# One list for the order of the first phase's products, and new durations for its small steps, in a fused attention and two-layer network kernel

## The chip, the core and the metric

The kernel runs on one core of one Trainium2 chip. A core has five engines with an instruction queue each: PE (TensorE, matrix products), DVE (VectorE), ACT (ScalarE), POOL (GpSimd) and SP (SyncE, which here only issues DMA transfers). Results of PE land in PSUM; the other engines take them from there into SBUF. The metric is the device time of one execution in microseconds (us); lower is better.

## What is computed

Eight batches of eight heads with 576 positions of 64 numbers; 32 packing rows per head. All data are 32-bit floats. Weights come as 64-bit numbers and are decoded on the chip.

```python
def sm_attn(qq, kk, vv):
    s = scale * np.matmul(qq, kk.transpose(0, 1, 3, 2))
    s = s - np.max(s, axis=-1, keepdims=True)
    a = np.exp(s)
    a = a / (np.sum(a, axis=-1, keepdims=True) + 1e-09)
    return np.matmul(a, vv)
p_packed = sm_attn(p, k, v)
out = sm_attn(q, p_packed, p_packed)          # then x: 4608 tokens x 512
...
h = np.maximum(np.maximum(x @ w1, x @ w2), x @ w3)     # 512 x 768 weights
x = h @ w_out                                          # 768 x 512
...
h = x @ w_in                                           # 512 x 2048
P = a[0] + a[1] * h + a[2] * h2 + a[3] * h3            # h2 = h*h, h3 = h2*h
Q = 1.0 + np.abs(b[0]) * np.abs(h) + np.abs(b[1]) * h2
out = (P / (Q + 1e-06)) @ w_out                        # 2048 x 512
```

## The kernel before

There are two phases. The second phase (lines 826 to 908) is the last layer, `psh` and `po` in the profile; the change does not touch it. The first phase does attention and the layer before it, and all its steps go through a planner.

**Steps of the first phase.** A unit `u` is one half batch of four heads; there are 16, four to a block `bp`. Each letter below is one small program step of `do()`:

- `S u` (`s_stage`, matrix products at line 469): scores of packing rows against k; then maximum, exponential and sums on DVE, ACT and POOL.
- `T u` (`a_stage`, line 513): four transposes of those weights. `V u` (`v_stage`, lines 532, 535 and, one transpose, 545): their product with v, which gives `ppk`, the packed rows.
- `s u` (`s2_stage`, line 560): scores of q against `ppk`, and their softmax on DVE, POOL and ACT, which ends in `a2h` and `a2l`, a high and a low part.
- `m` (`m_stage`, line 607): the packed rows times a 128-column piece of w1, w2 or w3, for two units; ACT and DVE split it in `mh` and `ml`. 48 of them. It needs the weight tile `wt`: in block 0 decoded from `w_raw` by DVE, ACT and POOL (lines 342 to 370), in later blocks loaded back from `w_scr`.
- `y` (`y_piece`, lines 59 to 61): twelve products of 288 columns, `a2` with `m`. 144 of them; three make one step of the maximum over w1, w2 and w3 (`hm`, lines 630 and 632), which `y_end` splits in `hh` and `hl`.
- `x` (`x2_stage`, lines 59 to 61 on `wo_h`): 36 products with w_out; 32 of them, the last eight outside the planner.
- `o`, `w`: decoding of a piece of w_out and of the second phase's weights.

**Two shapes on PE.** `y`, `x`, the transposes and the fillers use the whole 128x128 array. `S`, `s` and `m` use it as 64x32 tiles, the products with v as 128x32 tiles. Below, `S`, `s` and `m` are called tiled products; a run of tiled products with no whole-array product between them is called a visit to the tiled shape, and a tiled product that follows another one directly is called joined to it.

**What sets the order.** The steps are recorded in the order of a text of such letters, made by `text(bp)` from a table of places and by `m_next()`, which puts `m` a fixed number of steps ahead. `Plan.rate` gives every operation a due time from this order (for PE the sum of the durations before it). `Plan.run` then places operations on five modelled engines by readiness and due time; a PE operation may go ahead of the order by at most `AHEAD` = 12 us of due time. Durations (`us`) and a charge for a change of shape are numbers in the source. Where the modelled PE would wait over 0.3 us in the first 140 us, `keep_warm` puts transposes of an identity there, the fillers (line 285). PSUM holds two tiles `psy` (for `y`, `x` and fillers) and two tiles `pst` (for all small steps); `mh` and `ml` have four buffers each. What comes out is a fixed order for each engine.

Of the kernel before, what the change touches and what calls it, by code (L numbers as in the profile page):

```python
# [31 lines left out]
def attn_moe_moe2_kernel(  # L32
# [113 lines left out]
    class Plan:  # L146
# [51 lines left out]
        def run(self):  # L198
# [19 lines left out]
            for _ in range(len(self.ops)):  # L218
# [27 lines left out]
                op.eng, op.us = e, us  # L246
                if e == "PE":
                    if m != mode:
                        t, mode = t + 0.09, m
                    end = t + us + 0.18  # L250
                    free[e] = t + us
                elif e == "SP":
                    dma = max(dma, t + 2.7) + op.kb / 406.0
                    end, free[e] = dma, t + 0.45
                else:
                    if m == "two":
                        held[e] = t + us
                    end = t + us
                    free[e] = end - 0.08
# [33 lines left out]
    add = plan.add  # L293
# [6 lines left out]
    def flat(wt):  # L300
        return wt().rearrange("p a b -> p (a b)")[:, :768]

    def load_raw(src, up=0.0):

        n = src.shape[1]
        b = Buf(wp, [128, 768, 2] if wide else [128, 768], I32 if wide else F32, "w_raw", NRAW)

        def go():
            raw = b()[:, :n]
            nc.sync.dma_start(raw.rearrange("p n w -> p (n w)") if wide else raw, src.bitcast(I32) if wide else src)  # L310

        add("SP", 0, go, w=[b], kb=n, up=up)
        return b, n

    def decode(loaded, single, tiles, key):
# [72 lines left out]
    def w_decode(f, g, loaded):  # L388

        b = wt_buf()  # L390
        decode(loaded, True, lambda: (None, flat(b)), b)
        add("SP", 0, lambda: nc.sync.dma_start(w_scr[f, g], flat(b)), r=[b], w=[("w_scr", f, g)], kb=384)
        return b

    def w_load(f, g):

        b = wt_buf()
        add("SP", 0, lambda: nc.sync.dma_start(flat(b), w_scr[f, g]), r=[("w_scr", f, g)], w=[b], kb=384)
        return b
# [58 lines left out]
    def s_stage(u, kt):  # L458
# [33 lines left out]
                pool.tensor_tensor(out=s[a : a + 64, 3:4], in0=s[a : a + 64, i : i + 1], in1=s[a : a + 64, 2:3],  # L492
                                   op=ALU.add)

        add("PE", 0.58, mm, r=[kt, "pt"], w=[ps, e], mode="t")
        add("DVE", 0.75, lambda: dve.tensor_reduce(out=mx()[:, 0:2], in_=ps()[:, :, :288], axis=AX.X, op=ALU.max),
            r=[ps], w=[mx], up=OUT)
        add("DVE", 0.4, lambda: swap(dve), r=[mx], w=[mx], up=OUT, other={"POOL": (0.4, lambda: swap(pool), "two")})
# [6 lines left out]
    def a_stage(e):  # L505

        ps, at, ax = ps_buf("pst"), Buf(kp, [128, 4, 128], F32, "at", 2, False), Buf(kp, [128, 2, 32], F32, "ax", 3, False)

        def mm():
            for i in range(2):  # L510
                for c in range(2):
                    o = 320 * i + 128 * c
                    pe.transpose(ps()[:, 0, 256 * i + 128 * c : 256 * i + 128 * c + 128], e()[:, o : o + 128], ident)

        add("PE", 0.5, mm, r=[e], w=[ps, at])
        add("ACT", 0.6, lambda: act.copy(at().rearrange("p a b -> p (a b)"), ps()[:, 0]), r=[ps], w=[at], up=OUT)
        add("DVE", 0.2, lambda: dve.transpose(ax().rearrange("p a b -> p (a b)"), e()[:, 256:320]), r=[e], w=[ax])
        return at, ax

    def v_stage(u, at, vt, sm):  # L520
# [13 lines left out]
            for h in range(4):  # L534
                pe.matmul(pv[32 * h : 32 * h + 32, :64], lhsT=ax()[:, h // 2], rhs=vt()[:, 16 + h], start=False, stop=True)

        add("PE", 0.57, mm, r=[at, ax, vt], w=[ps], mode="v")

        def two():
            return ps()[:, 0, :64].unsqueeze(1).to_broadcast([128, 2, D])  # L540
# [9 lines left out]
    def s2_stage(u, qt, a2):  # L550
# [24 lines left out]
        def wide_of(t):  # L575
            return t().unsqueeze(2).to_broadcast([128, 18, 32])

        add("PE", 0.58, mm, r=[qt, ("ppk", u // 4 % 2, u % 4)], w=[ps, tb], mode="t")
        add("DVE", 0.9, turn, r=[ps], w=[tb], up=OUT)
        add("DVE", 0.75, lambda: dve.tensor_reduce(out=mx(), in_=t0(), axis=AX.X, op=ALU.max), r=[tb], w=[mx])  # L580
        add("POOL", 1.35, lambda: pool.tensor_tensor(out=t0(), in0=t0(), in1=wide_of(mx), op=ALU.subtract),
# [13 lines left out]
    def m_stage(bp, b2, wts):  # L595

        ps = ps_buf("pst")
        hi, lo = (Buf(mp, [128, 2, 384], F32R, f"m{x}", 4) for x in "hl")  # L600

        def mm():
            for g in range(2):
                for h in range(4):
                    i, j = divmod(h, 2)
                    l, c = slice(64 * j, 64 * j + 64), 32 * (h ^ g)
                    pe.matmul(ps()[c : c + 32, g, :384], lhsT=ppk[l, bp % 2, 2 * b2 + g, 32 * h : 32 * h + 32],  # L607
                              rhs=flat(wts[g])[l, 384 * i : 384 * i + 384], start=True, stop=True)

        add("PE", 0.74, mm, r=[*wts, ("ppk", bp % 2, 2 * b2), ("ppk", bp % 2, 2 * b2 + 1)], w=[ps, hi, lo], mode="t")  # L610
        add("ACT", 0.8, lambda: act.copy(hi(), ps()[:, :, :384]), r=[ps], w=[hi], up=OUT)
        add("DVE", 0.95, lambda: dve.tensor_tensor(out=lo(), in0=ps()[:, :, :384], in1=hi().bitcast(F32), op=ALU.subtract),
            r=[ps, hi], w=[lo], up=OUT)
        return hi, lo
# [60 lines left out]
    def a2_of(bp):  # L675
        return a2s.setdefault(bp, [[None, None], [None, None]])

    def m_next(n=1):
        for bp, f, b2 in m_seq[len(made) : len(made) + n]:
            if any(4 * bp + 2 * b2 + g not in vs for g in range(2)):  # L680
                break
            if (bp, f) not in wts:
                wts[bp, f] = [w_load(f, g) if bp else w_decode(f, g, load_raw(w123[2 * f + g], RUP.get(2 * f + g, 0.0))) for g in range(2)]
            ms[bp, f, b2] = m_stage(bp, b2, wts[bp, f])
            made.append((bp, f, b2))

    def y_steps():
        for bp in range(NBP):
            for k, (f, b2) in enumerate(YS[bp]):
                hm, h = hm_buf(), [Buf(hp_pool, [128, S], F32R, f"h{x}{b2}{f}") for x in "hl"]  # L690
                hs[bp][b2][f] = h
                for w in range(3):
                    if w == 1:
                        m_next(max(0, 12 * bp + min(k + MA, 12) - len(made)))
                    y_piece(w, ms[bp, f, b2], a2_of(bp)[b2], hm, h)
                    if w == 2:
                        y_end(hm, h)
                    yield
# [33 lines left out]
            if i is not None:  # L732
                w2_decode(i, load_raw(w_2[i]))

    def text(bp):
        at_ = {}

        def put(k, what):
            at_.setdefault(k, []).append(what)

        if bp + 1 < NBP:
            for u in range(4):
                for k, d in (("S", 0), ("T", 2), ("V", 3)):
                    put(PK[bp][u] + d, f"{k}{4 * bp + 4 + u}")
                put(S2AT[bp][u], f"s{4 * bp + 4 + u}")
            for k in MX[bp]:
                put(k, "m")
        for k in OAT if bp == 0 else WAT[bp]:
            put(k, "w" if bp else "o")
        out = START.split() if bp == 0 else []  # L750
        n = 36 - out.count("y")
        for k in range(36 - n, 44 if bp + 1 < NBP else 36):
            out += ["y" if k < 36 else "x"]
            out += at_.get(k, [])
        return out

    MA = 3
    RUP = {}
    START = "S0 S1 T0 T1 V0 V1 s0 s1 m S2 S3 T2 T3 V2 V3 s2 s3 m m"
    PK = [(16, 23, 30, 36), (2, 9, 16, 23), (2, 9, 16, 23)]  # L760
    S2AT = [(36, 37, 40, 41), (36, 37, 39, 40), (36, 37, 39, 40)]
    MX = [(38, 39)] * 3
    OAT = (28, 34, 37, 39)
    WAT = [(), (1, 5, 9, 13, 17, 21, 25, 29, 33, 36, 39, 41), (1, 5, 9, 13, 17, 21, 25, 29, 33, 36, 39, 41), (1, 5, 9, 13, 17, 21, 25, 29)]
    for bp in range(NBP):
        for what in text(bp):
            do(what)
    bp, hs = NBP - 1, hs[NBP - 1]

# [190 lines left out]
```

## Time and profile before

| | |
|---|---|
| median of 3 runs | 1319.13 us (1319.11 to 1319.16) |
| the profiled execution's own time | 1319.51 us |
| its span, first to last instruction | 1317.7 us |
| PE busy in the span | 1301.6 us, 99% |
| first `y` product starts | 41.18 us |
| first product of the second phase starts | 519.21 us |

The profile is of one execution. Spans, durations and waits are those of the hardware profiler; L469 is line 469 of the kernel. "Idle before" is the time that an engine stood still ahead of an instruction, and the arrow names what ended it. Ends of PE's products are modelled, since products are pipelined: one of 288 columns is shown as 0.29 us long while the next starts after 0.13 us.

### The profile page before, as it was taken

How to read it: one execution, taken by the hardware profiler on the slowest of the kernel's cores; microseconds unless marked ns; L12 is line 12 of the kernel's file. 1: busy time of each engine (PE TensorE's matmuls, PEld its weight loads, DVE VectorE, ACT ScalarE, POOL GpSimd, SP SyncE). 2: the span in 40 equal slices, each digit the busy share in tenths (PEclk: the TensorE clock that was granted, in tenths of full speed). 3: DMA queues.
4: the chain of work that ended last, by engine and by line, in shares of the span. 5: the costliest groups of instructions: out<-in, count | busy, mean ns of one | idle time of the engine just before them, and what ended most of it. 6: DMA issues, size and time to landing. Idle time of an engine off the chain costs nothing.

```text
span 1317.7 us, 21701 instructions
## 1 busy us (share of the span) xinstructions
PE 1301.6 (99%) x8582; PEld 1095.1 (83%) x8582; DVE 1059.4 (80%) x1652; ACT 798.5 (61%) x1346; POOL 218.0 (17%) x215
## 2 busy tenths in 40 slices
PE   9999999999999999999999999999999999999998
PEld 7878888998889899788888888888888888888886
DVE  6899878867886741999788888888897888888877
ACT  4465545435534422777668677686686776866765
POOL 4744523333233200001001010010010100100000
PEclk9999999999999999999999999999999999999999
DMA  9657656666646448501002001020020010100000
GB/s 377 255 192 250 211 193 233 227 216 217 228 134 231 139 165 312 218 6 43 17 0 64 1 17 49 0 64 1 0 65 0 17 41 0 56 1 0 33 1 33
DMA packets 52006, 141.92 MB, mean 108 GB/s; under 512 B 5568, under 2 KB 5568, under 8 KB 51136
## 3 DMA queue, kind: packets, MB, share of 16 engines
q1 hardware_dynamic: 51616, 140.01, 30.6%
q8 instruction: 67, 1.10, 0.3%
q10 hardware_dynamic: 288, 0.52, 0.1%
q14 instruction: 35, 0.29, 0.1%
HBM read 100.14 MB, written 40.37 MB: 107 GB/s over the span
## 4 chain that ended last, share of the span: by engine, by line
PE 75%; ACT 1%; DMA 1%; DVE 0%; issue 0%; POOL 0%; ACTq 0%
PE po L59 10%; PE po L60 10%; PE po L61 10%; PE psh L59 10%; PE psh L60 10%; PE psh L61 10%; PE psy L59 5%; PE psy L60 5%; PE psy L61 5%; PE pst L607 1%; DMA wt<-w_scr 0%; DMA w_scr<-wt 0%; PE pst L560 0%; PE pst L532 0%; DMA out_dram<-ob 0%
## 5 line engine op out<-in xcount | busy, mean ns | idle before, releaser
L59 PE MATMUL psh<-xh,wi_b 128*128 128x512 f32 x576 | 224.3, 390 | 1.0 <-issue 1.0
L60 PE MATMUL psh<-xl,wi_b 128*128 128x512 f32 x576 | 224.8, 391 | 0.0
L61 PE MATMUL psh<-xh,wi_b 128*128 128x512 f32 x576 | 224.4, 390 | 0.0
L59 PE MATMUL po<-wq_b,gh 128*128 128x512 f32 x540 | 212.2, 393 | 0.8 <-ACT gh L52 0.8
L60 PE MATMUL po<-wq_b,gh 128*128 128x512 f32 x540 | 211.2, 391 | 0.0
L850 ACT ACTIVATE hb<-psh,babs 128x512 f32<-128x512 f32 (+1 forms) x145 | 100.1, 690 | 177.7 <-PE psh L61 177.7
L853 DVE SCALAR_TENSOR_TENSOR hb<-h,babs,hb 128x512 f32<-128x512 f32 (+1 forms) x145 | 108.2, 746 | 97.3 <-ACT h L851 97.0
L61 PE MATMUL po<-wq_b,gl 128*128 128x512 f32 x540 | 182.2, 391 | 0.0
L59 PE MATMUL psy<-a2h,mh 128*128 128x288 f32 x576 | 177.4, 308 | 4.7 <-ACT hh L642 1.8
L60 PE MATMUL psy<-a2l,mh 128*128 128x288 f32 x576 | 169.8, 295 | 0.0
L61 PE MATMUL psy<-a2h,ml 128*128 128x288 f32 x576 | 169.7, 295 | 0.0
L56 POOL TENSOR_TENSOR xl<-xr,xh 128x512 fp32r<-128x512 f32 x28 | 37.0, 1320 | 641.8 <-ACT xh L52 641.8
L59 PEld LDWEIGHTS psy<-a2h,mh 128*128 128x128 f32 x576 | 108.2, 188 | 32.8 <-issue 10.9
L59 PEld LDWEIGHTS psh<-xh,wi_b 128*128 128x128 f32 x576 | 108.1, 188 | 24.6 <-issue 1.2
L61 PEld LDWEIGHTS psh<-xh,wi_b 128*128 128x128 f32 x576 | 108.1, 188 | 23.0
L60 PEld LDWEIGHTS psh<-xl,wi_b 128*128 128x128 f32 x576 | 108.2, 188 | 23.0
L61 PEld LDWEIGHTS po<-wq_b,gl 128*128 128x128 f32 x540 | 101.3, 188 | 23.8
L59 PEld LDWEIGHTS po<-wq_b,gh 128*128 128x128 f32 x540 | 101.4, 188 | 22.9 <-ACT gh L52 1.2
L60 PEld LDWEIGHTS po<-wq_b,gh 128*128 128x128 f32 x540 | 101.4, 188 | 22.4
L52 ACT CAST gh<-u 128x512 fp32r<-128x512 f32 (+1 forms) x145 | 90.7, 626 | 41.7 <-DVE u L860 40.4
L59 PE MATMUL psy<-hh,wo_h 128*128 128x288 f32 x384 | 115.4, 300 | 0.0
L858 DVE SCALAR_TENSOR_TENSOR u<-u,av,h 128x512 f32<-128x512 f32 (+1 forms) x145 | 108.7, 750 | 7.7 <-ACT h L855 7.6
(105 smaller groups left out, 2726.6 us busy)
## 6 DMA issues: line engine op xcount, KB each, us to landing
w_raw<-in_w_dram SPq DMA_DIRECT2D x32, 512.0 KB, 4.7
w_scr<-wt SPq DMA_DIRECT2D x32, 512.0 KB, 3.9
wt<-w_scr SPq DMA_DIRECT2D x36, 384.0 KB, 4.1
vraw<-in_v_dram SPq DMA_DIRECT2D x16, 640.0 KB, 5.3
kt<-in_k_dram SPq DMA_DIRECT2D x16, 576.0 KB, 6.1
w_raw<-in_w_dram SPq DMA_DIRECT2D x12, 768.0 KB, 8.5
kt<-in_q_dram SPq DMA_DIRECT2D x16, 576.0 KB, 6.0
x_scr<-hm SPq DMA_DIRECT2D x32, 288.0 KB, 3.3
```

What stands on the lines that cost most here:

```text
L52: act.copy(hi, src)
L56: e.tensor_tensor(out=lo, in0=src, in1=hi.bitcast(F32), op=ALU.subtract)
L59: pe.matmul(out_ap, lhsT=lh, rhs=rh, start=first, stop=False)
L60: pe.matmul(out_ap, lhsT=lh, rhs=rl, start=False, stop=False)
L61: pe.matmul(out_ap, lhsT=ll, rhs=rh, start=False, stop=last)
L607: pe.matmul(ps()[c : c + 32, g, :384], lhsT=ppk[l, bp % 2, 2 * b2 + g, 32 * h : 32 * h + 32], rhs=flat(wts[g])[l, 384 * i : 384 * i + 384] ...
L850: act.activation(hb, h, AF.Abs, scale=babs[:, 0:1])
L853: dve.scalar_tensor_tensor(out=hb, in0=h2, scalar=babs[:, 1:2], in1=hb, op0=ALU.mult, op1=ALU.add)
L858: dve.scalar_tensor_tensor(out=u, in0=u, scalar=av[:, 0:1], in1=h2, op0=ALU.add, op1=ALU.mult)
```

## The change

The places, the table and `text(bp)` go; in their stead stands one list of letters for the whole phase, `TEXT`, which a search program found by moving small steps about in the planner's model. `y_steps` no longer puts `m` in by itself, since the list holds all of them. The durations of seven kinds of PE steps in the model are set anew, and leaving the tiled shape has a charge of its own. Arithmetic, tiles, buffers and the second phase stay as they were.

```diff
                 if e == "PE":
                     if m != mode:
-                        t, mode = t + 0.09, m
+                        t += (0.13 if mode == "t" else 0.0) + (0.09 if m else 0.11)
+                        mode = m
...
-        add("PE", 0.58, mm, r=[kt, "pt"], w=[ps, e], mode="t")
+        add("PE", 0.51, mm, r=[kt, "pt"], w=[ps, e], mode="t")
...
-        add("PE", 0.5, mm, r=[e], w=[ps, at])
+        add("PE", 0.55, mm, r=[e], w=[ps, at])
...
-        add("PE", 0.57, mm, r=[at, ax, vt], w=[ps], mode="v")
+        add("PE", 0.6, mm, r=[at, ax, vt], w=[ps], mode="v")
...
-        add("PE", 0.58, mm, r=[qt, ("ppk", u // 4 % 2, u % 4)], w=[ps, tb], mode="t")
+        add("PE", 0.51, mm, r=[qt, ("ppk", u // 4 % 2, u % 4)], w=[ps, tb], mode="t")
...
-        add("PE", 0.74, mm, r=[*wts, ("ppk", bp % 2, 2 * b2), ("ppk", bp % 2, 2 * b2 + 1)], w=[ps, hi, lo], mode="t")
+        add("PE", 0.67, mm, r=[*wts, ("ppk", bp % 2, 2 * b2), ("ppk", bp % 2, 2 * b2 + 1)], w=[ps, hi, lo], mode="t")
...
-    def m_next(n=1):
-        for bp, f, b2 in m_seq[len(made) : len(made) + n]:
...
+    def m_next():
+        bp, f, b2 = m_seq[len(made)]
...
-            for k, (f, b2) in enumerate(YS[bp]):
+            for f, b2 in YS[bp]:
+                while (bp, f, b2) not in ms:
+                    m_next()
...
-                    if w == 1:
-                        m_next(max(0, 12 * bp + min(k + MA, 12) - len(made)))
...
-    START = "S0 S1 T0 T1 V0 V1 s0 s1 m S2 S3 T2 T3 V2 V3 s2 s3 m m"
-    PK = [(16, 23, 30, 36), (2, 9, 16, 23), (2, 9, 16, 23)]
...
+    TEXT = (
+        "S0 S1 T0 T1 V0 V1 m s0 S2 s1 S3 T3 T2 V3 V2 m s2 s3 m y m y y y m y m y y y y y S4 S6 m y y y y m y y y y y y",
...
+    for line_ in TEXT:
+        for what in line_.split():
             do(what)
```

Three places show what this moves. Lines of the changed file are one higher than before in this part (608 is 607 of before).

The first place is PE from just ahead of the first `y` to the wait in front of the thirteenth `y` before, and to the like wait after. L560 (561) is `s`, L607 (608) is `m`, L285 (286) a filler, L59 to L61 are `y`. Before:

```order
L560 MATMUL pst<-kt,ppk 32x288 x8
L545 MATMUL pst<-ident,zt 128x128
L285 MATMUL psy<-ident 128x128 x5
L560 MATMUL pst<-kt,ppk 32x288 x8
L285 MATMUL psy<-ident 128x128 x42
L59 MATMUL psy<-a2h_618,mh 128x288
...
L607 MATMUL pst<-wt,ppk 32x384 x16
L285 MATMUL psy<-ident 128x128 x42
```

After:

```order
L561 MATMUL pst<-kt,ppk 32x288 x16
L286 MATMUL psy<-ident 128x128 x12
L608 MATMUL pst<-wt,ppk 32x384 x16
L286 MATMUL psy<-ident 128x128 x13
L608 MATMUL pst<-wt,ppk 32x384 x8
L286 MATMUL psy<-ident 128x128 x9
L59 MATMUL psy<-a2h_647,mh 128x288
...
L286 MATMUL psy<-ident 128x128 x7
L608 MATMUL pst<-wt,ppk 32x384 x8
```

Ahead of the first `y` stand four `m` (32 instructions at L608 in all, one of the four further up) where one stood, and 209 fillers where 204 stood. After the first `y` stand 7 fillers, now after the sixth `y`, where 42 stood after the twelfth.

The second place is PE in the course of block 0, where S of the next block's units stands among `y` (L469, now L470). Before:

```order
L61 MATMUL psy<-a2h_906,ml 128x288
L469 MATMUL pst<-kt,pt 32x288 x8
L59 MATMUL psy<-a2h_618,mh 128x288
...
L61 MATMUL psy<-a2h_684,ml 128x288
L469 MATMUL pst<-kt,pt 32x288 x8
L59 MATMUL psy<-a2h_618,mh 128x288
```

After:

```order
L61 MATMUL psy<-a2h_751,ml 128x288
L470 MATMUL pst<-kt,pt 32x288 x8
L608 MATMUL pst<-wt,ppk 32x384 x8
L59 MATMUL psy<-a2h_647,mh 128x288
...
L61 MATMUL psy<-a2h_935,ml 128x288
L608 MATMUL pst<-wt,ppk 32x384 x16
L59 MATMUL psy<-a2h_955,mh 128x288
```

An `S` and an `m`, or two `m`, now go in one visit to the tiled shape. From the first `y` on there were 4 tiled products joined to another tiled one, and there are 26.

The third place is DVE around the first `y`. `dec_r`, `dec_t` and `wt` are the decoding of w1 to w3, `a2l` is what the first `y` waits for, `ml` belongs to an `m`, `hm` to a `y`. Before:

```order
L354 SCALAR_TENSOR_TENSOR wt<-w_raw,dec_r 128x768
L636 TENSOR_TENSOR a2l_685<-hm,a2h_684 128x576
L580 TENSOR_REDUCE mx_704<-e 128x18
L345 TENSOR_SCALAR dec_r<-w_raw 128x768
L632 TENSOR_TENSOR hm<-psy,hm 128x576
```

After:

```order
L613 TENSOR_TENSOR ml<-pst,mh 128x768 x2
L637 TENSOR_TENSOR a2l_752<-hm,a2h_751 128x576
L346 TENSOR_SCALAR dec_r<-w_raw 128x768
L343 TENSOR_SCALAR dec_t<-w_raw 128x768 x2
L355 SCALAR_TENSOR_TENSOR wt<-w_raw,dec_r 128x768
L346 TENSOR_SCALAR dec_r<-w_raw 128x768
L363 SCALAR_TENSOR_TENSOR dec_t<-w_raw,dec_t 128x768 x2
L633 TENSOR_TENSOR hm<-psy,hm 128x576
```

Nearly all of the fifth and sixth weight tiles' decoding on DVE now stands ahead of the first `hm` of a `y`; before, it began there and went on past the sixth `hm`.

## Rows read from the trace of the kernel before

**Rows 1.** Busy time of each engine by stretch of the span (us, instructions), granted PE clock.

```profile
0.00:41.20 41.20, 38.38 (x529) 30.45 (x529) 29.62 (x64) 18.20 (x39) 20.99 (x36) 1.00 0.97 385
41.20:126.00 84.80, 80.22 (x836) 68.67 (x834) 76.32 (x106) 48.94 (x81) 47.09 (x40) 1.00 0.62 218
126.00:250.00 124.00, 123.56 (x1294) 107.25 (x1293) 98.87 (x169) 61.04 (x110) 42.04 (x47) 1.00 0.63 211
519.20:1317.70 798.50, 791.68 (x3456) 648.54 (x3456) 673.27 (x1021) 561.88 (x935) 36.96 (x28) 1.00 0.10 33
```

**Rows 2.** Timeline of PE (start, length): one `m` alone, two `m` joined.

```profile
78.42 0.29 PE L60 MATMUL psy<-a2l,mh 128*128 128x288 f32 x1
78.55 0.29 PE L61 MATMUL psy<-a2h,ml 128*128 128x288 f32 x1
78.77 0.88 PE L607 MATMUL pst<-wt,ppk 64*32 64x384 f32 x16
79.57 0.40 PE L59 MATMUL psy<-a2h,mh 128*128 128x288 f32 x1
79.81 0.29 PE L60 MATMUL psy<-a2l,mh 128*128 128x288 f32 x1
...
44.32 0.29 PE L61 MATMUL psy<-a2h,ml 128*128 128x288 f32 x1
44.54 1.52 PE L607 MATMUL pst<-wt,ppk 64*32 64x384 f32 x32
45.99 0.40 PE L59 MATMUL psy<-a2h,mh 128*128 128x288 f32 x1
46.23 0.30 PE L60 MATMUL psy<-a2l,mh 128*128 128x288 f32 x1
```

**Rows 3.** Timeline of PE: the two long stretches of fillers.

```profile
36.62 4.80 PE L285 MATMUL psy<-ident 128*128 128x128 f32 x42
41.18 0.38 PE L59 MATMUL psy<-a2h,mh 128*128 128x288 f32 x1
...
66.59 4.80 PE L285 MATMUL psy<-ident 128*128 128x128 f32 x42
71.15 0.38 PE L59 MATMUL psy<-a2h,mh 128*128 128x288 f32 x1
```

**Rows 4.** All waits of PE, 41 to 519 us: total, times, longest.

```profile
PE psy L59 <- ACT hh L642: 1.8, 1, 1.8
PE psy L59 <- ACT hm L630: 1.6, 5, 0.7
PE psy L59 <- DVE hm L632: 1.2, 2, 0.8
PE pst L513 <- ACT e L483: 0.5, 1, 0.5
PE pst L532 <- ACT at L516: 0.3, 1, 0.3
```

**Rows 5.** Timeline of PE in the first 20 us, idle time in brackets.

```profile
1.42 4.32 PE L285 MATMUL psy<-ident 128*128 128x128 f32 x19 [1.42 <-POOL ident masks.py:199]
...
8.16 0.72 PE L469 MATMUL pst<-kt,pt 64*32 64x288 f32 x16 [0.73 <-DMA kt<-in_k_dram]
...
19.74 0.71 PE L560 MATMUL pst<-kt,ppk 64*32 64x288 f32 x13 [0.46 <-issue]
```

**Rows 6.** Timeline of DVE: one decoding step, twice.

```profile
61.14 0.95 DVE L354 SCALAR_TENSOR_TENSOR wt<-w_raw,dec_r 128x768 f32<-128x768 uint32 x1
...
64.40 2.19 DVE L354 SCALAR_TENSOR_TENSOR wt<-w_raw,dec_r 128x768 f32<-128x768 uint32 x1
```

**Rows 7.** Timeline of POOL at the same time.

```profile
64.35 1.42 POOL L636 TENSOR_TENSOR hl<-hm,hh 128x576 fp32r<-128x576 f32 x1
```

**Rows 8.** Groups of instructions: busy us, mean ns, idle before. What empties an `m`.

```profile
L612 DVE TENSOR_TENSOR ml<-pst,mh 128x768 fp32r<-128x768 f32 x48 | 45.5, 950 | 19.9 <-ACT mh L611 19.8
L611 ACT CAST mh<-pst 128x768 fp32r<-128x768 f32 x48 | 38.3, 800 | 25.1 <-PE pst L607 24.8
```

More of the change, by code (lines that the diff above doesn't have):

```diff
@@ L301, in flat, with load_raw @@
         return wt().rearrange("p a b -> p (a b)")[:, :768]
-    def load_raw(src, up=0.0):
+    def load_raw(src):
         n = src.shape[1]
@@ L310, in go @@
             nc.sync.dma_start(raw.rearrange("p n w -> p (n w)") if wide else raw, src.bitcast(I32) if wide else src)
-        add("SP", 0, go, w=[b], kb=n, up=up)
+        add("SP", 0, go, w=[b], kb=n)
         return b, n
@@ L676, in a2_of @@
         return a2s.setdefault(bp, [[None, None], [None, None]])
-    def m_next(n=1):
-        for bp, f, b2 in m_seq[len(made) : len(made) + n]:
[L680 to L685, printed above, removed]
+    def m_next():
+        bp, f, b2 = m_seq[len(made)]
+        assert all(4 * bp + 2 * b2 + g in vs for g in range(2))
+        if (bp, f) not in wts:
+            wts[bp, f] = [w_load(f, g) if bp else w_decode(f, g, load_raw(w123[2 * f + g])) for g in range(2)]
+        ms[bp, f, b2] = m_stage(bp, b2, wts[bp, f])
+        made.append((bp, f, b2))
     def y_steps():
         for bp in range(NBP):
-            for k, (f, b2) in enumerate(YS[bp]):
+            for f, b2 in YS[bp]:
+                while (bp, f, b2) not in ms:
+                    m_next()
                 hm, h = hm_buf(), [Buf(hp_pool, [128, S], F32R, f"h{x}{b2}{f}") for x in "hl"]
@@ L733, in do @@
                 w2_decode(i, load_raw(w_2[i]))
[L735 to L758, printed above, removed]
-    START = "S0 S1 T0 T1 V0 V1 s0 s1 m S2 S3 T2 T3 V2 V3 s2 s3 m m"
-    PK = [(16, 23, 30, 36), (2, 9, 16, 23), (2, 9, 16, 23)]
[L761 to L766, printed above, removed]
+    TEXT = (
[7 rows of a table added]
+    )
+    for line_ in TEXT:
+        for what in line_.split():
             do(what)
```

6 rows, old and new, of the table TEXT are left out of this document.

## The prediction, made before the changed kernel ran

> **What bounds the kernel now.** I read the stretches first. In every one of them PE is busy nearly throughout: 80.2 of 84.8 us from 41.2 to 126, 123.6 of 124.0 after it, 791.7 of 798.5 in the second phase [rows 1]. So PE sets the end from the first `y` on, and a change gains only what it takes out of PE's own queue: work, changes of shape, fillers, waits. The second phase, 798.5 us, is untouched and stays. What is at stake is the stretch from the first `y` at 41.18 [rows 3] to the start of the second phase at 519.2, and the start itself.
>
> Next I read what PE's waits come to there. The list of waits sums to 1.8 + 1.6 + 1.2 + 0.5 + 0.3 = 5.4 us in 10 waits [rows 4]. The view counts from the modelled end of a product, 0.29 us after its start, though the next could have started after 0.13 [rows 2]; with 0.16 for each of 10 that is 7.0 us. Fillers are counted as busy; the 42 in front of the thirteenth `y` fill 4.56 us, from 66.59 to 71.15 [rows 3], in which PE had nothing to do. So some 11.6 us of this stretch is standing still, and the rest is products and changes of shape.
>
> **The price of a visit to the tiled shape.** I read it from starts, since lengths overlap. One `m` alone: from the last `y` product ahead of it (78.55) to the second one behind it (79.81) are 1.26 us, of which two `y` products are 0.27, so the `m` costs 1.00. Two joined: 44.32 to 46.23 is 1.91, less 0.27 is 1.64, so the second costs 0.64 [rows 2]. A join thus saves 0.36. Of these, 0.20 are seen directly: the step into the `m` is 0.22 in place of 0.13, and the first product behind it takes 0.24 in place of 0.13; the other 0.16 is what stands between the last tiled product and the first whole one. A join of unlike products (`S` with `m`, `s` with `S`) is bounded by 0.20 and 0.36; since the one kind seen gives all of 0.36, I take 0.32 over all joins.
>
> **The change, part by part.**
>
> *Joins.* From the first `y` on the order has 26 tiled products joined to another in place of 4, 22 more. 22 x 0.32 = 7.0 us less (4.4 to 7.9). Joins with the product with v (128x32 tiles, another shape) are 4 before and 4 after and give nothing.
>
> *Three `m` ahead of the first `y`.* They leave the PE-bound stretch: 3 x 1.00 = 3.0 us less there. Ahead of the first `y` they stand where 42 fillers stood.
>
> *Fillers after the first `y`.* 42 become 7: 35 x 0.109 (4.56 / 42) = 3.8 us less, if the data is there. What the fillers covered was the fifth `m`, late because its two weight tiles were decoded late. After, both tiles' decoding stands ahead of the first `hm` on DVE, and that `m` stands on PE two `y` ahead of where the sixth `y` ends.
>
> *The first `y`.* In front of it are 3 more `m` (3 x 0.64 to 1.00, 1.9 to 3.0) and 5 more fillers (0.5): 2.4 to 3.5 later if PE stood still nowhere. Against that, the waits there can be taken up by the moved work: 0.73 for k's second transfer and 0.46 [rows 5]. That second k now goes behind a transfer of raw weights on SP's queue, which is about 0.79 MB at 385 GB/s [rows 1] = 2.0 us later, but 20 more fillers stand in front of its `S`. Between 0 and 3.5 later; I take 1.0, since what the first `y` waits for is a chain through DVE, ACT and POOL, and the order gives that chain about the same work as before but for two more `ml` (0.95 each [rows 8]) ahead of the last `a2l`, half of which I let hide in its gaps.
>
> *Waits.* Before they were 7.0. DVE is the one to fear. From 41.2 to 126 it was busy 76.3 of 84.8 us [rows 1], and part of that is standing still too: the same decoding step takes 0.95 at 61.14 and 2.19 at 64.40, and in the second case POOL ran a subtraction from 64.35 to 65.77 [rows 6, 7]; 65.77 plus 0.95 is 66.7, about the end of the slow one at 66.59. So the two exclude each other there. The Trainium skill says so too, in "SBUF — State Buffer", under "SBUF: two separate sides": GpSimd and VectorE share one port pair, as a lock held for the whole instruction. It speaks against this change: PE's stretch gets shorter and the locks in it don't. By that rule alone the stretch would keep its length, as in the first rival; by the idle time in the row it can shrink.
>
> How much is wanted of DVE here? PE stands still for 84.8 - 80.2 = 4.6 us of the stretch in the view, some 6 with the hidden 0.16 each, and 3.8 net of fillers go: 9.8 at most. (What the joins save here the new order spends: up to the 36th `y` it also holds a half `x`, an `s` and an `S` more.) DVE was idle for 8.5 us, and three `ml` (0.95 each [rows 8]) and at least two decoding steps (0.95 each [rows 6]) moved ahead of the first `y`, 4.7 us: 13.2 to give where 9.8 are wanted, though not all in the right place. I put the waits in this stretch at 7 us, and at 1.5 after it, where DVE has slack (98.9 of 124.0 busy [rows 1]): 8.5 in place of 7.0, bounds 2 and 12.
>
> *The rest.* The new durations in the model cost nothing themselves; they only act through the order. The eight last `x`, and the loads of the second phase's weights under them, stand as before.
>
> *Sum.* -7.0 - 3.0 - 3.8 + 1.0 + (8.5 - 7.0) = -11.3 us. From the profiled execution, 1319.5, that is 1308.2; the median of the runs lies 0.4 lower, so **1307.9**. Ends of the terms: joins 4.4 and first `y` 3.5 with 12 of waits give -2.7; joins 7.9, first `y` at 0 and waits of 2 give -19.7.
>
> **The rivals.**
>
> *DVE gives nothing.* The stretch up to the 36th `y` stays as long as it was because DVE, barred by POOL at times, is full. Then waits there are 9.8, 2.8 more than I take: -8.5, 1310.7. For it speak 76.3 of 84.8 us busy [rows 1]; against it the 4.7 us that left its list, and that POOL has no more work there than before, whose blocking the 76.3 already hold.
>
> *The clock.* The fillers keep PE from standing still. The first 19 took 0.227 us each, the 42 later 0.109 [rows 3, 5]: half speed, 1.2 in place of 2.4 GHz, at the start. With 7 fillers in place of 42 a wait that the planner does not foresee is left bare, and if the clock fell, as long a slow stretch as those 4.3 us would hold half the work: 2.2 us for each fall, -9.1 for one, 1310.1. Against it: 1.8 us of bare waiting [rows 4] left the granted clock at 1.00 [rows 1]. The Trainium skill, "TensorE: Matmul & The Clock Gate", under "What's actually happening", says that idle time brings the clock down by half; no row of this case after the start shows it.
>
> *Joined products wait for PSUM: slower.* Two `pst` tiles serve all small steps. A visit with two tiled products takes both, and the next small step must wait until ACT and DVE have emptied one: 0.80 + 0.95 = 1.75 us for an `m` [rows 8]. If each of the 26 joins costs PE such a wait in part, the gain is gone at 11.3 / 26 = 0.43 us each; at 1.0 us each the time is 1319.1 - 11.3 + 26 = 1334. Against it: the joined pair at 44.54 ran through without a gap [rows 2], and between visits there mostly stand one or more `y` of 1.6 us.
>
> *The new order does what it says and nothing waits.* Waits of 2 and a first `y` as early as before: -18.8, 1300.3. The model that places the steps now charges PE near what the rows show for a visit (0.09 + 0.67 + 0.13 + 0.11 = 1.00), where it charged 0.92. That the change does not reach PE's queue is excluded by the order itself.
>
> **How the numbers follow.** Chances: the sum as worked out (1303 to 1312.5) 0.67; DVE gives nothing 0.14; the clock 0.05; nothing waits (under 1303) 0.08; joins wait 0.06, of which half ends slower than before and the rest about the same or a little faster. The range holds the first three and the near half of the fourth: 1302.0 to 1313.5. 0.2% is 2.6 us, about what a measurement can tell here. Faster by more than that: 0.92; within it: 0.04; slower: 0.04.
>
> **What would show it.** In the profile after: the first `y` at 41 to 44 us; 216 fillers in all; the second phase's first product near 508, and 798.5 us from there to the end as before; lone `m` at 1.00 and joined ones near 0.64; waits of PE in between of some 6 to 9 us in the view, most of them ahead of 126 us and ended by DVE or ACT. I am wrong if PE waits at `pst` behind joined products, if the first `y` comes after 45, if the granted clock leaves 1.00, or if PE's waits past 126 us sum to over 4.

## The result, and the profile after

| | before | after |
|---|---|---|
| median of 4 runs each (lowest to highest), us | 1319.14 (1319.11 to 1320.06) | 1305.12 (1304.48 to 1306.58) |
| profiled execution: span / own time, us | 1317.7 / 1319.5 | 1304.7 / 1306.58 |
| first `y` starts / from there to the start of the last `x` product / second phase starts, us | 41.18 / 476.7 / 519.2 | 43.85 / 462.0 / 507.15 |

The ratio is 0.9894 [0.9876, 0.9911]: 14.0 us faster, where 11.2 were forecast, and inside the range (1302.0 to 1313.5). The middle number of the last row is called the stretch below: the part of the first phase in which PE sets the end, read from starts. The profiled execution happened to be the slowest of its four, by 1.3 us; so the traces have only 13.0 us of the difference. A part of the other 1.0 may lie at the start: in e3, e4 and e5 below, which have the same order on PE ahead of the first `y`, it comes at 44.08, 43.15 and 43.06, so a single trace fixes it to no better than 1 us.

Busy time by stretch, the answer to [rows 1] (columns as there: stretch, length, then PE, PEld, DVE, ACT, POOL busy, the granted clock, DMA share, GB/s):

```profile
43.80:126.00 82.20, 79.45 (x801) 69.64 (x800) 76.56 (x115) 48.08 (x82) 49.80 (x43) 1.00 0.58 212
126.00:250.00 124.00, 123.01 (x1330) 110.22 (x1331) 98.27 (x172) 59.99 (x106) 41.87 (x44) 1.00 0.63 213
507.10:1303.00 795.90, 791.70 (x3456) 648.58 (x3456) 673.25 (x1021) 561.89 (x935) 36.62 (x28) 1.00 0.10 33
```

PE is as full as it was (1288.8 us busy in the span, 99%), and the gaps that the view shows did not close, so time went because PE's queue got shorter; the fillers that went out of it had counted as busy. The second phase has the same 791.7 us of PE as before. DVE between the first `y` and 126 us is busy for 76.6 of 82.2 us, where it was for 76.3 of 84.8: nearly full, and still PE waits there for DVE's `hm` and `ml` for only 1.3 us.

The waits of PE from the first `y` to the last `x`, as [rows 4] (total, times, longest):

```profile
PE pst L608 <- DMA wt<-w_scr: 1.6, 1, 1.6
PE psy L59 <- DVE hm L633: 1.4, 3, 0.6
PE pst L608 <- DVE ml L613: 0.9, 1, 0.9
PE pst L608 <- ACT e L484: 0.8, 1, 0.8
PE psy L59 <- ACT hm L631: 0.7, 1, 0.7
```

They sum to 5.4 us in 7 waits, as much as before in 10. The long wait of a `y` for ACT `hh` is gone, and in its place `m` products wait at `pst`. The timeline of PE of the same kernel shows where (start, length, instructions, wait in brackets; one `m` is 16 records here, where the order in "The change" counts 8):

```profile
42.08 0.88 PE L608 MATMUL pst<-wt,ppk 64*32 64x384 f32 x16
42.89 1.20 PE L286 MATMUL psy<-ident 128*128 128x128 f32 x9
43.85 0.38 PE L59 MATMUL psy<-a2h,mh 128*128 128x288 f32 x1
...
53.61 0.29 PE L61 MATMUL psy<-a2h,ml 128*128 128x288 f32 x1
54.79 0.88 PE L608 MATMUL pst<-wt,ppk 64*32 64x384 f32 x16 [0.89 <-DVE ml L613]
...
66.90 0.29 PE L61 MATMUL psy<-a2h,ml 128*128 128x288 f32 x1
67.12 0.72 PE L470 MATMUL pst<-kt,pt 64*32 64x288 f32 x16
...
68.01 0.29 PE L60 MATMUL psy<-a2l,mh 128*128 128x288 f32 x1
...
72.53 0.29 PE L61 MATMUL psy<-a2h,ml 128*128 128x288 f32 x1
72.75 0.88 PE L608 MATMUL pst<-wt,ppk 64*32 64x384 f32 x16
74.38 0.88 PE L608 MATMUL pst<-wt,ppk 64*32 64x384 f32 x16 [0.76 <-ACT e L484]
...
75.43 0.30 PE L60 MATMUL psy<-a2l,mh 128*128 128x288 f32 x1
...
95.53 0.29 PE L61 MATMUL psy<-a2h,ml 128*128 128x288 f32 x1
95.75 0.72 PE L470 MATMUL pst<-kt,pt 64*32 64x288 f32 x16
96.26 0.85 PE L608 MATMUL pst<-wt,ppk 64*32 64x384 f32 x16
...
97.28 0.29 PE L60 MATMUL psy<-a2l,mh 128*128 128x288 f32 x1
...
104.45 0.29 PE L61 MATMUL psy<-a2h,ml 128*128 128x288 f32 x1
104.67 1.52 PE L608 MATMUL pst<-wt,ppk 64*32 64x384 f32 x32
106.12 0.40 PE L59 MATMUL psy<-a2h,mh 128*128 128x288 f32 x1
106.36 0.30 PE L60 MATMUL psy<-a2l,mh 128*128 128x288 f32 x1
...
321.28 0.29 PE L61 MATMUL psy<-a2h,ml 128*128 128x288 f32 x1
323.13 2.43 PE L608 MATMUL pst<-wt,ppk 64*32 64x384 f32 x32 [1.56 <-DMA wt<-w_scr]
325.49 0.40 PE L59 MATMUL psy<-a2h,mh 128*128 128x288 f32 x1
325.73 0.29 PE L60 MATMUL psy<-a2l,mh 128*128 128x288 f32 x1
```

The pair at 104.67 is read as in [rows 2]: from 104.45 to 106.36 are 1.91, less 0.27 for two `y` products 1.64. So the join saves 0.36, as before the change. The `S` joined with an `m` at 95.75 is read the same way: 95.53 to 97.28 is 1.75, less 0.27 is 1.48, and a lone `S` is 0.84 (66.90 to 68.01, less 0.27), so the join saves 0.84 + 1.00 - 1.48 = 0.36: a join of unlike products saves as much. Of the 26 joined pairs, 21 stand between whole-array products of `y` or `x`; the 19 of them without a wait save 0.35 to 0.36 each. The rows at 72.75 and 74.38 are the one joined pair that waits in its middle for a PSUM tile: from 72.53 to 75.43 it took 1.0 more than the pair at 104.67. At 323.13 two `m` in one visit ask for a weight tile that is still being loaded, and from 321.28 to 325.73 the pair took 4.18 in place of 1.64, so that wait cost 2.54 where the view shows 1.56. The lone `m` at 54.79 waits for the `ml` of an `m` that ran at 42.08: it stood in its PSUM tile until DVE came to that `ml` at 53.70.

DVE ahead of the first `y` (same kernel, its timeline):

```profile
40.88 1.82 DVE L613 TENSOR_TENSOR ml<-pst,mh 128x768 fp32r<-128x768 f32 x2
42.62 0.75 DVE L637 TENSOR_TENSOR a2l<-hm,a2h 128x576 fp32r<-128x576 f32 x1
```

The two `ml` fill DVE up to the last `a2l` (L637), which the first `y` needs. It ends at 43.37, and the `y` starts at 43.85 right behind its fillers.

### The profile page after: what moved, and what is told of

Read it like the earlier page. It is cut to its first block, busy times and chain, and to the rows that moved or that the text cites. A ratio compares the mean times of both kernels' runs of the same rounds, so it can differ in the third digit from the quotient of the medians.

```text
span 1304.7 us, 21631 instructions
## 1 busy us (share of the span) xinstructions
PE 1288.8 (99%) x8552; PEld 1094.0 (84%) x8552; DVE 1043.2 (80%) x1648; ACT 799.4 (61%) x1346; POOL 224.6 (17%) x219
## 4 chain that ended last, share of the span: by engine, by line
PE 92%; DMA 3%; DVE 3%; ACT 1%; POOL 0%; issue 0%; SPq 0%; POOLq 0%; ACTq 0%; DVEq 0%
PE po L59 10%; PE po L60 10%; PE po L61 10%; PE psh L59 10%; PE psh L60 10%; PE psh L61 10%; PE psy L59 9%; PE psy L60 9%; PE psy L61 9%; PE pst L608 2%; DMA w_scr<-wt 1%; DMA vraw<-in_v_dram 1%; PE psy L286 1%; DMA kt<-in_k_dram 1%; PE pst L561 1%; DMA wt<-w_scr 1%
## 5 line engine op out<-in xcount | busy, mean ns | idle before, releaser
L59 PE MATMUL psh<-xh,wi_b 128*128 128x512 f32 x576 | 224.3, 390 | 1.0 <-issue 1.0
L61 PE MATMUL psh<-xh,wi_b 128*128 128x512 f32 x576 | 224.4, 390 | 0.0
L59 PE MATMUL po<-wq_b,gh 128*128 128x512 f32 x540 | 212.1, 393 | 0.8 <-ACT gh L52 0.8
L61 PE MATMUL po<-wq_b,gl 128*128 128x512 f32 x540 | 182.2, 391 | 0.0
L59 PE MATMUL psy<-a2h,mh 128*128 128x288 f32 x576 | 175.7, 305 | 1.4 <-ACT hm L631 0.7
L61 PE MATMUL psy<-a2h,ml 128*128 128x288 f32 x576 | 169.7, 295 | 0.0
L59 PEld LDWEIGHTS psh<-xh,wi_b 128*128 128x128 f32 x576 | 108.2, 188 | 24.6 <-issue 1.2
L61 PEld LDWEIGHTS psh<-xh,wi_b 128*128 128x128 f32 x576 | 108.1, 188 | 23.0
L59 PEld LDWEIGHTS psy<-a2h,mh 128*128 128x128 f32 x576 | 108.1, 188 | 19.9 <-issue 6.9
L61 PEld LDWEIGHTS po<-wq_b,gl 128*128 128x128 f32 x540 | 101.3, 188 | 23.8
L59 PEld LDWEIGHTS po<-wq_b,gh 128*128 128x128 f32 x540 | 101.4, 188 | 22.9 <-ACT gh L52 1.2
L59 PE MATMUL psy<-hh,wo_h 128*128 128x288 f32 x384 | 114.6, 298 | 0.6 <-DVE hm L633 0.6
```

Of the source, the lines that this page charges most:

```text
L59: pe.matmul(out_ap, lhsT=lh, rhs=rh, start=first, stop=False)
L61: pe.matmul(out_ap, lhsT=ll, rhs=rh, start=False, stop=last)
```

## The experiments

All numbers are medians, with the 95% interval of the ratio to the kernel before, which ran beside each group of runs (1319.14 beside the kernel after, 1320.00 beside e1 to e4, 1319.56 and 1319.57 beside the others; so a difference between groups carries up to 0.9 us of the runs' own scatter). Where a trace is spoken of, "stretch" is the time from the first `y` to the start of the last `x` product: 476.7 us before, 462.0 after. The kernels leave nothing of the computation out; e3 and e4 add transposes that nobody reads, and e7 and e9 leave out fillers only.

### The two halves of the change apart

*e1_durations* is the kernel before with the new durations and the new charge for a change of shape, in the old order of steps:

```diff
-                        t, mode = t + 0.09, m
+                        t += (0.13 if mode == "t" else 0.0) + (0.09 if m else 0.11)
+                        mode = m
...
-        add("PE", 0.74, mm, r=[*wts, ("ppk", bp % 2, 2 * b2), ("ppk", bp % 2, 2 * b2 + 1)], w=[ps, hi, lo], mode="t")
+        add("PE", 0.67, mm, r=[*wts, ("ppk", bp % 2, 2 * b2), ("ppk", bp % 2, 2 * b2 + 1)], w=[ps, hi, lo], mode="t")
...
```

Expected: 

> The order of before, with only the planner's new durations and charges for a change of shape. Theory of visits (the gain is taken out of PE's own queue: joined tiled products, three m moved ahead of the first y, fillers that are no longer needed): the order made by the planner still has 4 joins after the first y and one m ahead of it, and 52 fillers in place of 42, so nothing is gained: 1318.5 to 1320.5 us. Rival (the new durations make the planner place DVE's and DMA's work better, and the list adds little): 1308 to 1313 us, with waits of PE gone.

Measured: 1319.52, ratio 0.9995 [0.9985, 1.0004]; first `y` at 41.38, stretch 476.8. The durations alone do nothing.

*e2_list* is the other half: the new list, with the old durations and charge. From its first `y` on it has 26 joined products like the kernel after, but the planner puts only one of the four `m` ahead of the first `y`, and 43 fillers behind it.

```diff
-                        t += (0.13 if mode == "t" else 0.0) + (0.09 if m else 0.11)
-                        mode = m
+                        t, mode = t + 0.09, m
...
-        add("PE", 0.67, mm, r=[*wts, ("ppk", bp % 2, 2 * b2), ("ppk", bp % 2, 2 * b2 + 1)], w=[ps, hi, lo], mode="t")
+        add("PE", 0.74, mm, r=[*wts, ("ppk", bp % 2, 2 * b2), ("ppk", bp % 2, 2 * b2 + 1)], w=[ps, hi, lo], mode="t")
```

Expected: 

> The new list with the old durations. The planner makes of it 26 joins after the first y, as in the changed kernel, but one m ahead of the first y in place of four and 43 fillers after it in place of 7. Theory of visits: only the joins are paid out, 22 x 0.32 = 7.0 us from before, and the first y comes about when it did before (203 fillers ahead of it): 1311 to 1314 us. Rival (joins are worth little, the gain is in the fillers and waits): 1317 to 1319 us. Second rival (the list does it all): 1305 us.

Measured: 1313.89, ratio 0.9954 [0.9939, 0.9968]; first `y` at 40.70, stretch 471.6. The list alone gives 6.1 us, the durations alone 0.5, both together 14.0: they are worth more together, since with the old durations the planner does not carry out the list's `m` ahead of the first `y`, and with the new ones it does. What these `m` are worth by themselves is measured in e8 below; which of the durations lets them through was not tested.

### What a change of shape costs

*e3_split* puts one identity transpose (128x128, into a part of the PSUM tile that nobody reads) ahead of each of the 26 joined products after the first `y`, which undoes the joins and nothing else.

```diff
+                    broken[0] = m == "t" and mode == "t" and t > 40.0
                     if m != mode:
...
+    def part(ps):
+        if broken[0]:
+            pe.transpose(ps()[:, 1, 384:], ident, ident)
...
         def mm():
+            part(ps)
...
```

Expected: 

> The changed kernel with one transpose of the identity, into a free part of the same PSUM tile, in front of each of the 26 tiled products after the first y that are joined to another; nothing else moves on any engine. Theory of visits: each costs its own 0.11 us and undoes a join of 0.32 (0.20 to 0.36): 26 x 0.43 = 11.2 us more (8 to 12.2), 1313 to 1317.5 us. Rival (changes of shape overlap with waits, the gain is elsewhere): 26 x 0.11 = 2.9 us more, 1308 us.

*e4_nosplit* puts the same transpose ahead of 42 tiled products that are joined to nothing, where it parts nothing:

```diff
+                    broken[0] = m == "t" and mode == "" and t > 40.0
```

Expected: 

> Control for the split: the same transpose in front of each of the 42 tiled products after the first y that follow a whole-array product, so that no change of shape is added. Both theories: 42 x 0.11 = 4.6 us more less what stands in a wait anyway, 1308.5 to 1310 us. If it costs as much as in the split (0.43 each, 18 us, 1323 us), the price is not that of the shape.

Measured: e3 1314.64, ratio 0.9958 [0.9943, 0.9973], 9.5 us above the kernel after; e4 1309.23, ratio 0.9920 [0.9903, 0.9936], 4.1 above (8.7 and 3.3 if each is counted from the kernel before beside it). In the traces the stretch grows by 8.0 us (470.0) and by 3.4 (465.4), and of the wait of 1.6 us for a weight tile nothing is left in e3 and 0.7 in e4, so the transposes cost 9.6 / 26 = 0.37 each where they part a join, and 4.2 / 42 = 0.10 where they don't. The difference, 0.27, is a mean over joins of all kinds. The timeline of PE in e3 shows the same pair as at 104.67 in the kernel after:

```profile
104.81 0.29 PE L61 MATMUL psy<-a2h,ml 128*128 128x288 f32 x1
105.04 0.88 PE L618 MATMUL pst<-wt,ppk 64*32 64x384 f32 x16
105.84 0.33 PE L288 MATMUL pst<-ident 128*128 128x128 f32 x1
106.10 0.88 PE L618 MATMUL pst<-wt,ppk 64*32 64x384 f32 x16
106.91 0.40 PE L59 MATMUL psy<-a2h,mh 128*128 128x288 f32 x1
107.15 0.29 PE L60 MATMUL psy<-a2l,mh 128*128 128x288 f32 x1
```

104.81 to 107.15 is 2.34, less 0.27 for two `y` products 2.07, where the joined pair took 1.64: 0.43 for the transpose and the second visit. With 0.109 for the transpose, as for a filler, the visit is 0.32. Both are low readings: two lone `m` are 2.00 and the parted pair is 2.07, so between two visits the transpose adds only 0.07, and 0.43 - 0.07 is the 0.36 that the rows of the kernel after give. The Trainium skill, "TensorEngine Tiling (Array Packing)", "Key Properties", says that a change of the tiling mode drains TensorE; a price of 0.36 us for each visit fits that, though no row shows the drain itself.

### Where along the way it comes from

*e5_new_then_old* has the new list up to the 36th `y` and the old order from there, with 6 joins in all; *e6_old_then_new* has them the other way round, with 24.

```diff
...
-        "y T6 y T4 y m V4 y y y m S5 T5 y m m y y V5 y y y y s5 o S7 y y o x y x x T7 m V7 V6 w o s7 s4 o x x x x x y",
+        "y y y m y y y y y y y T6 y T4 y m V4 y y y m S5 T5 y m m y y V5 y y y y s5 o S7",
+        "y y o x y V6 s4 x o x T7 m x V7 m o x s6 x s7 x x y m y w y S8 y m y T8 y V8 w y",
...
```

```diff
-        "S0 S1 T0 T1 V0 V1 m s0 S2 s1 S3 T3 T2 V3 V2 m s2 s3 m y m y y y m y m y y y y y S4 S6 m y y y y m y y y y y y",
...
+        "S0 S1 T0 T1 V0 V1 s0 s1 m S2 S3 T2 T3 V2 V3 s2 s3 m m y y y y m y y y m y y y m y y y m",
...
```

Expected of e5: 

> The changed kernel up to the 36th y (block 0), then the remaining steps in the order of before, with the new durations. 6 joins after the first y in place of 26; four m ahead of the first y and 7 fillers after it, as in the changed kernel. Theory of visits: 20 joins are lost, 20 x 0.27 to 0.36 = 5.4 to 7.2 us more than the changed kernel: 1310 to 1312.5 us. Rival (the gain is all in block 0, where PE stood still): 1305 to 1306.5 us.

Expected of e6: 

> The order of before up to the 36th y, then the remaining steps in the order of the list. 24 joins after the first y, one m ahead of it, 52 fillers after it. Theory of visits: 20 joins more than before, 5.4 to 7.2 us less than 1319.5: 1312 to 1314.5 us; with the run of the other half the two gains sum to that of the whole, 14 us. Rival (all in block 0): 1318 to 1319.5 us.

Measured: e5 1312.00, ratio 0.9942 [0.9927, 0.9957]; e6 1313.02, ratio 0.9950 [0.9935, 0.9965]. Against the runs of the kernel before beside them (1319.56) the first half gives 7.6 us and the second 6.5: 14.1, the whole. For e6 the kernel to compare with is e1, which has the same order up to the first `y` and the same 52 fillers after it: 1319.52 to 1313.02 is 6.5 as well, with 20 products joined, 6.5 / 20 = 0.33 each (0.30 by the traces, whose stretch is 6.0 shorter). From the other side, e5 is 6.9 above the kernel after with 20 joins less, 0.34 each (0.30 by the traces, 468.0 against 462.0). PE's waits in the view differ among these runs by up to 1 us, so the runs bear the price out and don't sharpen it.

### The `m` ahead of the first `y`

*e8_m_behind* is the kernel after with three `m` behind the second `y` in the list. One `m` then stands ahead of the first `y` and 34 fillers after it, and there are 29 joins.

```diff
-        "S0 S1 T0 T1 V0 V1 m s0 S2 s1 S3 T3 T2 V3 V2 m s2 s3 m y m y y y m y m y y y y y S4 S6 m y y y y m y y y y y y",
+        "S0 S1 T0 T1 V0 V1 m s0 S2 s1 S3 T3 T2 V3 V2 s2 s3 y y m m m y y m y m y y y y y S4 S6 m y y y y m y y y y y y",
```

Expected: 

> The changed kernel with the three m that stood ahead of the first y put behind it in the list (two of them right behind the second y). The planner then has one m ahead of the first y, 197 fillers ahead of it and 34 behind it, and no ml of theirs ahead of the last a2l on DVE. Theory of visits: the first y comes about when it did before, 41 to 42 us (2 to 2.7 earlier), the three m go back into PE's full stretch (2.6 to 3.0 more) and 27 fillers are 2.9 more: 1307.5 to 1310 us. Rival (the later first y of the changed kernel is a loss that nothing pays back): 1302.5 to 1303.5 us.

Measured: 1311.70, ratio 0.9939 [0.9922, 0.9956], 6.6 us above the kernel after (5.5 in the traces at the start of the second phase); the expectation was missed on the slow side. Its first `y` is 3.4 us earlier (40.49), but the 36 `y` of block 0 then take 87.9 us, first start to last start, where they took 78.1 (behind them it wins back 0.9). The list of PE's waits from 40 to 126 us in e8:

```profile
PE psy L286 <- DVE hm L633: 3.1, 1, 3.1
PE psy L59 <- ACT hm L631: 1.6, 2, 1.1
PE psy L59 <- DVE hm L633: 1.4, 2, 1.0
```

These are 6.1 us, where the kernel after has 2.8 in the same stretch (0.9 + 0.8 + 0.7, and 0.4 of the waits for `hm`). What the longest of them does is in the stretches around it, and in the timeline of PE:

```profile
55.00:58.00 3.00, 1.10 (x32) 0.39 (x32) 3.00 (x5) 1.78 (x3) 1.58 (x1) 1.00 0.22 57
58.00:60.00 2.00, 0.81 (x4) 0.81 (x5) 1.90 (x4) 1.20 (x2) 2.00 (x2) 0.70 1.01 388
60.00:65.00 5.00, 5.00 (x34) 5.00 (x33) 4.84 (x10) 2.20 (x7) 2.97 (x3) 0.78 0.84 286
65.00:70.00 5.00, 4.48 (x54) 3.12 (x53) 4.70 (x9) 2.92 (x8) 4.07 (x7) 1.00 0.64 233
```

```profile
54.90 1.20 PE L470 MATMUL pst<-kt,pt 64*32 64x288 f32 x32
59.20 3.31 PE L286 MATMUL psy<-ident 128*128 128x128 f32 x15 [3.09 <-DVE hm L633]
62.26 0.38 PE L59 MATMUL psy<-a2h,mh 128*128 128x288 f32 x1
62.48 0.29 PE L60 MATMUL psy<-a2l,mh 128*128 128x288 f32 x1
62.60 0.29 PE L61 MATMUL psy<-a2h,ml 128*128 128x288 f32 x1
```

Behind the wait the granted clock falls from 1.00: 0.70 from 58 to 60 us and 0.78 from 60 to 65, that is a time at 1.2 GHz. The 15 fillers take 3.06 us from start to start (59.20 to 62.26), 0.20 each, where 15 at full speed take 1.64: the loss is 1.4 us. The `y` products right behind them follow at 0.12 to 0.13 us again, at full speed. So of the 9.8 us, 3.0 are the three `m`, 27 x 0.109 = 2.9 the fillers at full speed, 3.3 waits behind DVE and ACT, 1.4 the clock, and -1.1 three joins more (3 x 0.36): 9.5. I had not counted the waits and the clock. Here an `m` that is made late is paid for by more than its own 1.0 us.

### The fillers and the clock

*e7_no_fillers* is the kernel after without any filler, *e9_fewer* has 161 ahead of the first `y` where 209 stand, and 5 after it where 7 stand.

```diff
-    COLD, WARM, KEEP = 8.0, 140.0, 0.3
+    COLD, WARM, KEEP = 8.0, 140.0, 1e9
```

```diff
-                        keep_warm(int((wait - 0.1) / (0.215 if t < COLD else 0.11)))
+                        keep_warm(int((wait - 0.1) / (0.215 if t < COLD else 0.11) * (1.0 if t < 12.0 else 0.7)))
```

Expected of e7: 

> The changed kernel without any filler: 216 transposes of the identity that keep PE at work are left out. If the fillers only fill time, the first y comes when DVE's a2l is there, at 43.4 us or a little earlier, and the time is 1304 to 1305 us. If they hold PE's clock up, the granted clock shows a lower level at the start, PE's small steps ahead of the first y take up to twice as long (S 0.65, T 0.44, V 0.7, four of each and of s and m, some on the chain of two units), the first y comes 2 to 5 us later and the first of the y run at half speed: 1307 to 1312 us.

Expected of e9: 

> The changed kernel with 0.7 of its fillers from 12 us on (161 ahead of the first y in place of 209, 5 behind it in place of 7), nothing else moved. If the fillers ahead of the first y hold it up, it comes up to 48 x 0.11 = 5 us earlier; if DVE's a2l bounds it (done at 43.37, the y at 43.85), it gains at most 0.4 us: 1304.5 to 1305.2 us, as long as the granted clock stays up. If gaps of a third bring the clock down, 1306 to 1308 us as without fillers.

Measured: e7 1308.19, ratio 0.9910 [0.9895, 0.9925], 3.1 us above the kernel after. Some of its first stretches, and the timeline of PE:

```profile
20.00:30.00 10.00, 7.34 (x116) 2.96 (x100) 8.39 (x18) 6.21 (x11) 3.93 (x7) 1.00 1.02 416
...
35.00:40.00 5.00, 3.66 (x73) 2.09 (x74) 3.60 (x8) 2.06 (x6) 4.03 (x3) 0.50 1.01 403
...
43.00:45.00 2.00, 1.02 (x25) 0.18 (x16) 1.95 (x3) 1.57 (x4) 1.70 (x2) 0.92 1.01 416
```

```profile
5.49 1.21 PE L470 MATMUL pst<-kt,pt 64*32 64x288 f32 x16 [5.49 <-DMA pt<-in_p_dram]
...
22.57 1.54 PE L608 MATMUL pst<-wt,ppk 64*32 64x384 f32 x16 [1.38 <-DVE e L569]
...
40.83 2.72 PE L608 MATMUL pst<-wt,ppk 64*32 64x384 f32 x32
44.53 0.88 PE L608 MATMUL pst<-wt,ppk 64*32 64x384 f32 x16 [0.98 <-DVE ml L613]
45.34 0.40 PE L59 MATMUL psy<-a2h,mh 128*128 128x288 f32 x1
```

The granted clock is at half, 1.2 GHz, from 35 to 40 us. An `m` takes 1.54 and a pair 2.72 where they take 0.88 and 1.52 at 2.4 GHz. PE worked with hardly a pause from 38.52 to 43.5, and the next `m` is at full speed again. Even so the first `y` comes only 1.5 us later (45.34) and runs at full speed, and the stretch grows by 0.4 to 462.4: PE has slack ahead of the first `y`, so half speed there costs little. The time lies in the range expected for a lower clock, but the 2 to 5 us and the slow first `y` expected with it did not come; and of the 3.1 us the traces show 1.9.

e9: 1304.74, ratio 0.9885 [0.9872, 0.9899], not to be told apart from the kernel after. Its first `y` starts at 42.42, 0.6 to 1.7 us earlier than in the four traces with all fillers (43.06 to 44.08), though 48 x 0.109 = 5.2 us of PE's work were left out. It is the lowest median of all, but 0.4 us is within what the runs scatter, so it is not called a better version.

### A try at a better start

*e10_k_first* loads the second k ahead of the first raw weights on SP's queue, since the kernel after waits 0.97 us for it. The planner then puts 223 fillers ahead of the first `y`.

```diff
-    def load_raw(src):
+    def load_raw(src, up=0.0):
...
-        add("SP", 0, go, w=[b], kb=n)
+        add("SP", 0, go, w=[b], kb=n, up=up)
...
+    RUP = {0: -6.0}
```

Expected: 

> The changed kernel with the first transfer of raw weights put back on SP's queue, so that the second k comes ahead of it as before the change, and the order of the start as the planner then makes it (223 fillers ahead of the first y in place of 209; the rest after the first y as in the changed kernel). If the first y is late because the second k is (its S waits 0.97 us), it comes at 42 to 43 us: 1303.5 to 1304.5 us. If DVE's work ahead of the last a2l (two ml more) makes it late, it stays at 43.5 to 45: 1304.8 to 1306 us.

Measured: 1308.13, ratio 0.9915 [0.9901, 0.9928], 3.0 us worse than the kernel after; the expectation was missed. The first `y` is at 45.65, 1.8 later, and the stretch is 1.1 shorter. The trace accounts for only 0.7 of the 3.0 by the start of the second phase (507.80); the rest stays open, as its profiled execution was the fastest of its five and that of the kernel after the slowest of its four.

## Why the prediction was right, step by step

| term, us | predicted | measured |
|---|---|---|
| joins | -7.0 (0.32 each) | -8.1 (22 at 0.36, read directly, are 7.9) |
| three `m` ahead of the first `y` | -3.0 | -3.0 (counted at the price before) |
| fillers after the first `y` | -3.8 | -3.8 (42 to 7) |
| waits in the stretch | +1.5 | +0.2 |
| sum, the stretch | -12.3 | -14.7 |
| first `y` | +1.0 | +2.7 (1.9 to 2.9 over four traces) |
| behind the last `x` | 0 | -1.0 in the span |
| in all | -11.3 | -13.0 in the span, -14.0 in the medians |

The forecast time came out well in part by luck: the joins and the waits were each better than forecast by 1.1 to 1.3 us and the span behind the last `x` by 1.0, and the first `y` was worse by 1.7.

The stretch (476.7 to 462.0) and the first `y` are read from starts. So are the waits: the three at `pst` cost 2.54 (at 323.13), 1.0 (at 74.38) and 0.96 (at 54.79: 53.61 to 55.84 is 2.23, less 0.27 and the `m`'s own 1.00), and the four of whole-array products are 2.1 in the view and 0.16 more each; that is 7.2, against 7.0 before, as good as unchanged. The `m` and the fillers are counted at their price before; what is left, -14.7 + 3.0 + 3.8 - 0.2 = -8.1, is put down to the joins. It is 8.1 / 22 = 0.37 each, and the rows of the kernel after give 0.36 by themselves.

*Joins* were sized a little too small. "A join thus saves 0.36" was right and holds for unlike products too; taking 0.32 over all joins was the error, and 7.9, the upper end that I gave, is what the rows show. The other readings lie lower (0.27 and 0.32 from e3, 0.30 to 0.34 from e5 and e6); each of them carries other waits or the price of a transpose with it.

*The first `y`* was the term that I sized too small. "Half of which I let hide in its gaps" failed: the two `ml` stand whole, 1.82 us from 40.88 on, ahead of the last `a2l` on DVE, in a row without a gap. The bound of 3.5 held it. That PE's own queue does not set the time is supported by e9, where 48 fillers less bring the first `y` only 0.6 to 1.7 us earlier. That the two `ml` do is not shown by themselves, since e8 takes them and three `m` of PE away together.

*Waits* were sized too large, 8.5 for 7.2, and in the wrong places. Ahead of 126 us I put 7; the rows give 3.4 (2.8 in the view). Past 126 I put 1.5; they give 3.9 (2.6 in the view), of which 2.5 are the two `m` at 323 us that wait for a weight tile, a wait that I had not named. The sign "some 6 to 9 us in the view, most of them ahead of 126 us" thus failed (5.4, about half), while "over 4" past 126 us was not reached. The wait for DVE that I feared did not come: DVE had 8.5 us idle in its stretch [rows 1] and has 5.6 left, though that stretch got 6.6 us shorter up to the 36th `y` (84.75 to 78.10, start to start). It also lost less time beside POOL: of the decoding steps that take 0.95 alone, two took 2.19 and 2.23 before, and after the change the slowest took 1.52 (at 85.98, beside a POOL subtraction from 84.54 to 86.68) and 1.14. "DVE gives nothing" falls with that.

*The clock* stayed at 1.00 in all stretches with 7 fillers in place of 42. That the fillers matter at all is shown by e7: without them PE runs at half speed up to 43 us. What a fall after the first `y` costs is shown by e8, 1.4 us, where I had 2.2; it came there behind a bare wait of 3.1 us, while behind the longest in the kernel after, 1.6, the granted clock stayed at 1.00.

*Joined products wait for PSUM.* By "I am wrong if PE waits at `pst` behind joined products" this rival did show itself, but once, 1.0 us at 74.38. 26 joins at 0.43 were needed to spend the gain; the parted pairs of e3 confirm that joining pays.

*The interaction* was not in the prediction as such: e1 and e2 give 6.6 together and the whole change 14.0. I took the order as given, in which the durations have already acted, so the sum came out right without it. e8 shows what hangs on the three `m`: 5.5 to 6.6 us, of which "3.0", a share of "3.8" and the first `y` were in my terms, and the waits and the clock were not.

*The second phase* starts at 507.15 (forecast: near 508), and from there to its last product it takes 792.87 us in both kernels. The 0.9 to 1.0 us behind it (the span less the last product's start is 5.6 before and 4.7 after) was forecast at nothing. It is not shown to come from the change: the same time is 5.2 in e1 and 5.1 in e6, and 4.7 in e5, which has the old order from block 1 on.

## What to carry to other kernels

Where one engine is full, price the change of shape from starts of its neighbours and count how often the order pays it: here 22 changes less were over half of what the stretch got shorter, and no row of idle time showed them. Work that can go ahead of the stretch that sets the end can be worth more than its own length if other engines must digest its result: three products of 1.0 us each, put back, cost some 6 us. With the old durations the planner here did not carry out the order that the search had found, so change the two together and test them apart.

## What I had not expected of the hardware

The record of the granted clock in e7 begins at 1.00 and stays there to 30 us, while an `m` at 22.57 took 1.54 us, as at the half speed that the record shows only from 35 us on. An `S` at 5.49 took 1.21 in place of 0.72 [rows 5]: PE was slow from its first product on, and the durations show it where the record does not. The Trainium skill, "TensorE: Matmul & The Clock Gate", "What's actually happening", says that the throttled state is the default and activity releases it; the durations agree with that, the record's first 30 us do not.

48 of 209 fillers ahead of the first `y` can go at no measurable cost (e9, 0.4 us lower), while all of them together are worth 3.1 us (e7, 1.9 of it in the traces).
